# The first 480 words of a hand-written order, written anew, in an attention and gMLP kernel

## The chip, the core and the metric

The kernel runs on one core of a Trainium2 chip. The metric is the device time of one execution in microseconds (us). Six engines of the core work beside each other, each through its own list of instructions in order: TensorE (PE in the profile, its weight loads PEld), VectorE (DVE), ScalarE (ACT), GpSimd (POOL), SyncE (SP, which here only issues DMAs), and the DMA engines. They wait for each other by semaphores.

## What is computed

Attention over 8 batches of 12 heads, 448 positions and 64 dimensions, with q and k normalised by their root mean square, and behind it one gated block with a product over positions:

```
q_n, k_n = rmsnorm(q, g_q), rmsnorm(k, g_k)
attn = softmax(q_n @ k_n.T / 8);  x = attn @ v          # heads side by side: 8 x 448 x 768
h = relu(x @ w_in);  u, v = h[..., :512], h[..., 512:]
v_n = (v - mean(v)) / sqrt(var(v) + 1e-6)
out = (u * (w_spatial @ v_n + b_spatial)) @ w_out       # 8 x 448 x 768
```

Inputs and output are float32; the products are made in bf16 and summed in float32.

## The kernel before

A group G is four heads of one batch, so there are 24 groups, three to a batch. Nothing is scheduled by a program: `PLAN` is one string of 1632 words, and a loop at the end of the kernel function walks it and calls for each word the function `op_` of its first letter. A word reads name.arguments/slots/engine: `Q.1.1/2/g` squares k of group 1 (the last argument 0 is q, 1 is k) into buffer 2 on POOL (g; a is ACT, v DVE). Each engine runs its instructions in the order of the words that land on it, so the string decides what stands behind what.

The words that matter here, with the lines of the instructions:

- `l`, `L` (L306, L302): load a half of group 0's q or k, or q or k of another group, into one of nine buffers `raw`, issued by SP. `v`, `ws`, `wb`, `wo`, `wi` load v and the weights, issued by POOL. `g` loads a gain, issued by ACT.
- `q`, `Q` (L391 on DVE and POOL, L389 on ACT): squares. `r`, `R` (L409, L403, DVE only): row sums of the squares. `i`, `j` and `I`, `J` (L432, L435, L418, L425, ACT): the reciprocal root by a logarithm and an exponential. `n`, `N` (L450, L442): the normalised rows `nrm`. Small letters are the halves of group 0.
- `p`, `P` (L469, L461, PE): seven transposes by the identity into a PSUM bank. `k`, `K` (L372, L370 for q, L480, L478 for k with the gains): the copy out of it into `qT` or `kT`. From group 4 on `T` (L497), a DMA transpose, and `Z` take their place.
- `S.G.u` (L523, PE): two blocks of scores into two banks. With `f` it is four matmuls of 64 columns of weights, without it eight of 32. `E.G.u` (L532, ACT): the exponential of these two blocks into one of 21 buffers `et`; seven to a group.
- `s`, `a`, `b` (L558, PE): the sums of the exponentials and the two halves of their product with v. With a last argument 1 a word does two groups, eight matmuls. `D`, `d` (L577, L581, ACT) and `X` (L587, DVE) divide.
- `V`, `W`, `U` (L603, L637, L677, PE): products with w_in, and `c`, `u`, `B`, `H`, `G`, `O`, `o`, `t` the rest of the block.
- `Y`, `y` (L357 on PE, L372 on DVE or L370 on ACT): w_spatial transposed and copied. `gA` (L376, DVE), `gB` (L381, PE), `gC` (L384, DVE): the product of the two gains, turned into a column.
- `z.n.w` (L269, PE): n idle units, matmuls of the identity that nobody reads. Of them w times four make one wide matmul of 512 columns; the rest are narrow ones of 128 columns, or of 64 where the slot is `e`.

Operations of DVE and POOL that go through `port` (squares, norms, some copies) wait for the last such operation of the other engine that stands ahead of them in the plan. The order of the plan is kept on every engine, also where an operand comes late.

## Time and profile before

| | |
|---|---|
| runs | 265.84, 266.46, 266.88 us; median 266.46 |
| profiled execution | 268.54 us in all, span 266.7 us |
| mean granted TensorE clock | 0.985 |
| DMA | 51.08 MB, mean 192 GB/s |
| chain that ended last | PE 66%, DMA 11%, DVE 8%, ACT 7% |

The span goes from the first to the last instruction of the profiled execution. A busy PE says that some matmul was under way, not that it went at full speed. In the rows below, a time with a length is the start of a group of instructions and how long they took together, x the count, and in brackets the idle time of the engine ahead of them and what ended it. Where instructions of one engine overlap at their ends, the start of the next is the better measure of a length than the end.

### The profile page before, as it was taken

The page shows a single profiled execution, that of the slowest core. Times are in us where ns is not written, and L with a number is a line of the kernel's source. Part 1 is how long each engine was busy: PE and PEld are TensorE (multiplying, and loading weights), DVE is VectorE, ACT ScalarE, POOL GpSimd, SP SyncE. Part 2 cuts the span into 40 slices and gives each one's busy share as a digit, 9 for nine tenths or more (in the row PEclk, how much of TensorE's full clock was granted, in tenths as well). Part 3 has the DMA queues.
Part 4 walks back from the last instruction along what each step waited for, and adds up shares of the span by engine and source line. Part 5 has one row for each costly group of instructions (what it writes and reads, how often), then busy time and mean ns, then how long its engine had stood idle before and what let it go on. Part 6 is the DMA issues. An engine that isn't in the chain of part 4 may idle for free.

```text
span 266.7 us, 9428 instructions
## 1 busy us (share of the span) xinstructions
PE 254.9 (96%) x4025; PEld 129.4 (49%) x4041; DVE 213.3 (80%) x368; ACT 216.8 (81%) x357; POOL 127.5 (48%) x109
## 2 busy tenths in 40 slices
PE   7989999999999999999999999999999999999993
PEld 2454435434545456454455454454455555455561
DVE  4899799998698999979799988898983564476861
ACT  1788999999999999997899999997989983332522
POOL 3686246778874789267888577518210000000000
PEclk9995999999999999999999999999999999999999
DMA  6999997999999999999999999999952051031136
GB/s 194 328 306 312 225 258 98 161 232 222 147 233 288 226 240 187 329 204 186 238 240 223 211 248 182 180 196 264 228 115 118 2 209 32 2 124 57 29 158 227
DMA packets 62690, 51.08 MB, mean 192 GB/s; under 512 B 39160, under 2 KB 58808, under 8 KB 62648
## 3 DMA queue, kind: packets, MB, share of 16 engines
q1 hardware_dynamic: 54304, 42.02, 63.4%
q0 software_dynamic: 8192, 8.27, 20.2%
q8 instruction: 31, 0.51, 0.8%
q10 hardware_dynamic: 152, 0.20, 0.2%
q14 instruction: 11, 0.09, 0.1%
HBM read 38.55 MB, written 11.01 MB: 186 GB/s over the span
## 4 chain that ended last, share of the span: by engine, by line
PE 66%; DMA 11%; DVE 8%; ACT 7%; POOL 4%; issue 3%; SPq 0%; POOLq 0%; DVEq 0%
PE ps L558 13%; PE ps L677 11%; PE ps L523 10%; PE ps L713 10%; PE ps L603 9%; PE ps L691 7%; ACT et L532 5%; DMA raw<-in_q_dram 5%; PE ps L637 3%; DMA qT<-nrm 3%; DMA kr<-nrm 3%; POOL nrm L442 3%; DVE xt L587 1%; DVE ss L403 1%; POOL sqt L391 1%
## 5 line engine op out<-in xcount | busy, mean ns | idle before, releaser
L532 ACT ACTIVATE et<-ps 128x896 bf16<-128x896 f32 x168 | 145.3, 923 | 8.1 <-PE ps L523 7.3
L442 POOL TENSOR_TENSOR nrm<-raw,rs 128x896 bf16<-128x896 f32 x32 | 53.7, 1690 | 23.8 <-ACT rs L425 7.3
L391 POOL TENSOR_TENSOR sqt<-raw 128x896 f32<-128x896 f32 (+1 forms) x28 | 46.1, 1650 | 35.4 <-DVE sqt L391 20.1
L523 PE MATMUL ps<-qT,kT 64*32 64x448 bf16 (+1 forms) x1060 | 59.2, 361 | 2.7 <-DMA qT<-nrm 0.6
L403 DVE TENSOR_REDUCE ss<-sqt 128x14 f32<-128x896 f32 x46 | 49.0, 1077 | 1.2 <-POOL sqt L391 1.0
L558 PE MATMUL ps<-et,vt 64*32 64x448 bf16 x1344 | 44.8, 350 | 0.0
L677 PE MATMUL ps<-xt,w_in 128*128 128x448 bf16 x192 | 43.8, 353 | 0.1
L523 PEld LDWEIGHTS <-kT 64*32 64x32 bf16 (+1 forms) x1060 | 21.6, 94 | 33.6 <-issue 21.6
L713 PE MATMUL ps<-w_out,gt 128*128 128x384 bf16 (+1 forms) x196 | 37.5, 323 | 0.1
L603 PE MATMUL ps<-w_in,xt 128*128 128x512 bf16 x128 | 35.6, 380 | 1.0 <-issue 0.3
L587 DVE TENSOR_TENSOR xt<-ps,rc 128x448 bf16<-128x448 f32 x48 | 27.6, 615 | 7.8 <-PE ps L558 6.5
L370 ACT ACTIVATE os<-ps 128x384 f32<-128x384 f32 (+3 forms) x34 | 15.8, 477 | 16.1 <-PE ps L713 12.3
L558 PEld LDWEIGHTS <-vt 64*32 64x32 bf16 x1344 | 22.3, 92 | 12.0 <-issue 3.5
L691 PE MATMUL ps<-w_spT,vn 128*128 128x448 bf16 (+1 forms) x128 | 27.7, 353 | 0.1
L677 PEld LDWEIGHTS <-w_in 128*128 128x128 bf16 x192 | 17.5, 98 | 19.8 <-issue 5.3
L323 POOL DMA_DIRECT2D vt<-in_v_dram x36 | 24.0, 668 | 6.5 <-PE ps L523 6.5
L558 PE MATMUL ps<-et,ones 64*32 64x448 bf16 x672 | 25.9, 353 | 0.4 <-ACT et L532 0.4
L713 PEld LDWEIGHTS <-gt 128*128 128x128 bf16 x196 | 18.3, 98 | 16.0 <-issue 2.8
L372 DVE COPY os<-ps 128x384 f32<-128x384 f32 (+3 forms) x33 | 17.3, 535 | 10.7 <-PE ps L713 6.7
L696 DVE TENSOR_TENSOR gt<-ps,us 128x448 bf16<-128x448 f32 x32 | 19.5, 622 | 6.9 <-PE ps L691 6.1
L652 DVE BATCH_NORM_STATS2 s<-vs 128x6 f32<-128x512 bf16 (+1 forms) x32 | 21.8, 682 | 1.6 <-ACT vs L594 1.4
L603 PEld LDWEIGHTS <-xt 128*128 128x128 bf16 x144 | 12.7, 97 | 16.7 <-issue 5.4
(61 smaller groups left out, 255.8 us busy)
## 6 DMA issues: line engine op xcount, KB each, us to landing
raw<-in_k_dram SPq DMA_DIRECT2D x23, 448.0 KB, 6.1
raw<-in_q_dram SPq DMA_DIRECT2D x23, 448.0 KB, 5.7
out_dram<-os SPq DMA_DIRECT2D x23, 384.0 KB, 3.1
vt<-in_v_dram POOLq DMA_DIRECT2D x24, 112.0 KB, 5.8
vt<-in_v_dram POOLq DMA_DIRECT2D x12, 224.0 KB, 7.4
out_dram<-os SPq DMA_DIRECT2D x9, 192.0 KB, 4.3
w_in<-in_moe_w_in_dram POOLq DMA_DIRECT2D x1, 1536.0 KB, 14.1
w_out<-in_moe_w_out_dram POOLq DMA_DIRECT2D x4, 192.0 KB, 4.5
```

The source lines that it names most:

```text
L323: pool.dma_start(out=vts[b % 2][64 * halves[0]:64 * halves[0] + 64 * len(halves), g].rearrange("p r c d -> p r (c d)"), in_=src)
L391: port(eng, eng.tensor_tensor(out=t, in0=x, in1=x, op=ALU.mult))
L403: dve.tensor_reduce(out=sss[where["ssl", pair[G]]][:, G - pair[G], i].rearrange("p r c -> p (r c)"), in_=sqt[where.pop(("sq", G, i))].rear ...
L442: port(eng, eng.tensor_tensor(out=nrm[sl[0]].rearrange("p c r d -> p r c d"), in0=raw[where["raw", G, i]].rearrange("p r (c d) -> p r c d" ...
L523: pe.matmul(out=ps[at:at + w, sl[n], 0:S], lhsT=kT[64 * r:64 * r + 64, c, 64 * hh + x:64 * hh + x + w], rhs=qT[64 * r:64 * r + 64, :, 64 * ...
L532: act.activation(out=ets[sl[0]].rearrange("k n (p c) -> k n p c", c=C), in_=ps[:, a:a + 2, 0:S].rearrange("k n (c p) -> k n p c", p=T), fu ...
L558: pe.matmul(out=ps[32 * l:32 * l + 32, where[kind, G][0], 0:S], lhsT=w, rhs=et_of(G, r, c)[at:at + 64], start=(n == 1), stop=(n == C), til ...
L587: dve.tensor_tensor(out=xts[b % 2][:, 2 * g + half, :], in0=ps[:, where.pop(("ab"[half], G))[0], 0:S], in1=rcs[where["rc", G]], op=ALU.mult)
L603: pe.matmul(out=ps[:, bank, :], lhsT=xts[b % 2][:, j, 128 * m:128 * m + 128], rhs=w_in[:, j // 2, j % 2, DH:], start=(n == 1 and j == 2 * ...
L677: pe.matmul(out=ps[:, bank, 0:S], lhsT=w_in[:, j // 2, j % 2, 128 * f:128 * f + 128], rhs=xts[b % 2][:, j, :], start=(n == 1 and j == 2 * ...
L691: pe.matmul(out=ps[:, sl[0], 0:S], lhsT=vns[b % SLOTS["vn"]][rows, m, 128 * f:128 * f + 128], rhs=w_spT[rows, m, :], start=(m == 0), stop= ...
L713: pe.matmul(out=ps[:, sl[0], 0:n], lhsT=gts[b % 2][:, f, 128 * m:128 * m + 128], rhs=w_out[:, f, x:x + n], start=(f == 0), stop=(f == 3))
```

## The change

The first 480 or so words of `PLAN` are in another order; from word 486 on the names and engines are the same, with other buffer numbers. No function changes. The same operations are done, except for the idle units: `z.72.18`, twice `z.16.4`, `z.21.0`, `z.8.0` and `z.3.0` go, and `z.60.15`, `z.6.1`, `z.12.3`, `z.30.0`, `z.42.0` and `z.8.2` come, so 21 wide ones instead of 26, and 74 narrow ones instead of 32. 25 words change their engine or form, among them `n.1.0`, `n.1.1`, `n.0.1` (DVE to POOL), `k.1.1` (ACT to DVE), `k.1.0` (DVE to ACT), `k.0.0` (ACT to DVE), `Q.2.0` (POOL to ACT), `Q.1.0` (ACT to POOL), `Q.1.1` (POOL to ACT), `y.2` (DVE to ACT) and `N.1.0` (DVE to POOL). The start of the string:

```diff
-setup//v l.1.0/0 l.0.0/1 l.0.1 g.1//a g.0//a l.1.1 L.1.1/2 q.0.0/0/v r.0.0//v L.1.0/3 L.2.1/4 q.1.0/1/g r.1.0//v wb//g
-L.2.0/5 i.0//a j.0//a n.0.0//v z.72.18/0 p.0.0/0 q.1.1//a ws//g gA//v q.0.1//a k.0.0/0/a L.3.1/6 gB/7 n.1.0//v p.1.0/6
...
+setup//v l.1.0/0 l.0.0/1 l.1.1 g.0//a g.1//a l.0.1 L.1.1/2 q.0.0/0/v q.1.0/1/g r.0.0//v L.1.0/3 wb//g L.2.1/4 ws//g
+r.1.0//v q.1.1//a r.1.1//v i.0//a j.0//a n.0.0//v L.2.0/5 gA//v z.60.15/0 gB/0 L.5.0/6 q.0.1//a r.0.1//v gC//v L.3.1/7
...
```

What this does to ACT where the exponentials begin. Before, from the square of q of group 1 on (`et` with its number is an exponential, `kT0` the second half's copy of k, `ls` and `rs` the two small operations of group 1's norm):

```order
L389 ACTIVATE sqt1_74<-raw3_67 128x896
L532 ACTIVATE et0_90<-ps_63 128x896
L478 ACTIVATE kT0_86<-ps_63,g2_col_162 64x896
L532 ACTIVATE et1_91<-ps_63 128x896
L418 ACTIVATE ls0_116<-ss0_113,eps_157 128x28
L425 ACTIVATE rs0_119<-ls0_116 128x28
L532 ACTIVATE et2_92<-ps_63 128x896
```

Now, from the first half's copy of k on:

```order
L478 ACTIVATE kT0_86<-ps_63,g2_col_162 64x896
L389 ACTIVATE sqt0_73<-raw2_66 128x896
L532 ACTIVATE et0_90<-ps_63 128x896
L532 ACTIVATE et1_91<-ps_63 128x896
L532 ACTIVATE et2_92<-ps_63 128x896
L532 ACTIVATE et3_93<-ps_63 128x896
L418 ACTIVATE ls0_116<-ss0_113,eps_157 128x28
L425 ACTIVATE rs0_119<-ls0_116 128x28
L389 ACTIVATE sqt1_74<-raw5_69 128x896
L532 ACTIVATE et4_94<-ps_63 128x896
```

Four exponentials now stand in a row ahead of the norm of group 1, and the copy between the first two is gone.

DVE at the same place, before, from the copy of the gains on (`nrm01` and `nrm00` are the second halves' norms of group 0, `ss0` the row sums of group 1 and `ss1` those of group 2):

```order
L384 COPY g2_col_162<-ps_63 128x1
L480 TENSOR_SCALAR kT0_86<-ps_63,g2_col_162 64x896
L450 TENSOR_TENSOR nrm01_126<-raw0_64,rs0_124 128x448
L450 TENSOR_TENSOR nrm00_125<-raw1_65,rs0_124 128x448
L403 TENSOR_REDUCE ss0_113<-sqt2_75 128x14
L372 COPY qT0_80<-ps_63 64x896
L403 TENSOR_REDUCE ss0_113<-sqt1_74 128x14
L403 TENSOR_REDUCE ss1_114<-sqt0_73 128x14
```

Now:

```order
L384 COPY g2_col_162<-ps_63 128x1
L372 COPY qT0_80<-ps_63 64x896 x2
L480 TENSOR_SCALAR kT0_86<-ps_63,g2_col_162 64x896
L403 TENSOR_REDUCE ss0_113<-sqt0_73 128x14
L403 TENSOR_REDUCE ss0_113<-sqt1_74 128x14
L403 TENSOR_REDUCE ss1_114<-sqt2_75 128x14
```

Three copies out of PSUM now stand ahead of the first row sum of group 1, the norms have left the engine, and no row sum stands between the copies.

POOL, before, from its first load of v on:

```order
L323 DMA vt0_127<-in_v_dram 64x2x448
L391 TENSOR_TENSOR sqt2_75<-raw2_66 128x896
L343 DMA w_out_153<-in_moe_w_out_dram 128x768
L391 TENSOR_TENSOR sqt0_73<-raw4_68 128x896
L391 TENSOR_TENSOR sqt2_75<-raw5_69 128x896
```

Now:

```order
L323 DMA vt0_127<-in_v_dram 128x2x448
L450 TENSOR_TENSOR nrm01_126<-raw0_64,rs0_124 128x448 x2
L450 TENSOR_TENSOR nrm00_125<-raw1_65,rs0_124 128x448
L391 TENSOR_TENSOR sqt1_74<-raw3_67 128x896
L391 TENSOR_TENSOR sqt2_75<-raw4_68 128x896
L442 TENSOR_TENSOR nrm0_76<-raw3_67,rs0_119 128x2x7x64
```

Three half norms of group 0 have come to POOL, ahead of its squares, and one of its three squares has gone to ACT.

## The prediction

> **What bounds the kernel now.** I read the page's list of engines first, then the busy time by stage, then the engines in order of time up to 46 us, because the change touches nothing behind its 485th of 1632 plan words.

> ```profile
> PE 254.9 (96%) x4025; PEld 129.4 (49%) x4041; DVE 213.3 (80%) x368; ACT 216.8 (81%) x357; POOL 127.5 (48%) x109
> ```

> TensorE is the bound on average, but an average hides the stages. The next rows are the busy times by stage: for each stretch its length, then the busy time of PE, PEld, DVE, ACT and POOL, the granted clock, and the DMA's share and rate.

> ```profile
> 0.00:12.00 12.00, 9.70 (x50) 3.92 (x50) 7.00 (x20) 5.12 (x10) 5.90 (x12) 1.00 0.84 259
> 12.00:26.69 14.69, 13.42 (x193) 7.72 (x197) 13.58 (x19) 12.47 (x18) 10.89 (x9) 0.77 1.13 306
> 26.69:45.65 18.96, 17.43 (x465) 8.81 (x454) 17.52 (x22) 18.87 (x33) 7.39 (x7) 1.00 0.95 197
> 45.65:100.00 54.35, 54.06 (x892) 25.75 (x897) 49.21 (x88) 52.83 (x84) 42.11 (x34) 1.00 1.06 217
> ```

> From 45.65 to 100 us PE idles for 0.29 us, so whatever moves 45.65 moves the end by about as much. Ahead of it the bound is another: from 26.69 to 45.65 ACT idles for 0.09 us (18.96 less 18.87) and PE for 1.53. So I follow ACT's exponentials to 45.65, where the first matmul on w_in starts:

> ```profile
> 12.00 0.92 ACT L532 ACTIVATE et<-ps 128x896 bf16<-128x896 f32 x1 [0.30 <-PE ps L523]
> 12.94 1.00 ACT L478 ACTIVATE kT<-ps,g_col 64x896 bf16<-64x896 bf16 x1
> 15.30 0.32 ACT L418 ACTIVATE ls<-ss,eps 128x28 f32<-128x28 f32 x1 [0.41 <-DVE ss L403]
> 15.78 2.51 ACT L532 ACTIVATE et<-ps 128x896 bf16<-128x896 f32 x3
> 19.39 0.94 ACT L389 ACTIVATE sqt<-raw 128x896 f32<-128x896 f32 x1
> 20.23 3.55 ACT L532 ACTIVATE et<-ps 128x896 bf16<-128x896 f32 x4
> 23.93 0.92 ACT L532 ACTIVATE et<-ps 128x896 bf16<-128x896 f32 x1 [0.15 <-PE ps L523]
> 25.32 0.92 ACT L532 ACTIVATE et<-ps 128x896 bf16<-128x896 f32 x1 [0.47 <-PE ps L523]
> 26.57 2.73 ACT L532 ACTIVATE et<-ps 128x896 bf16<-128x896 f32 x3 [0.33 <-PE ps L523]
> 41.88 0.92 ACT L532 ACTIVATE et<-ps 128x896 bf16<-128x896 f32 x1
> ...
> 43.60 2.12 PE L558 MATMUL ps<-et,vt 64*32 64x448 bf16 x80
> 45.65 2.76 PE L603 MATMUL ps<-w_in,xt 128*128 128x512 bf16 x11
> ```

> Of the 28 exponentials of groups 0 to 3, nine are done at 23.78 (20.23 + 3.55), the last at 42.80, and 2.85 us later the w_in matmuls start. In a row each costs 0.80 ((2.51 - 0.92) / 2, three of them without the last one's length), and the two small operations of a norm cost 0.48 (15.30 to 15.78). I count 18.87 us from 23.93 to 42.80 for 19 exponentials and nine small operations, with 0.80 of waits for PE (0.47 + 0.33).

> Those waits have a cause. PE ran at half the clock from 19.86 to 26.69 us. I cut the time around it into pieces half as long as this stretch:

> ```profile
> 16.45:19.86 3.41, 2.33 (x53) 1.75 (x50) 3.11 (x5) 2.76 (x6) 3.39 (x5) 1.00 1.09 324
> 19.86:23.27 3.41, 3.33 (x40) 2.06 (x39) 2.86 (x5) 3.29 (x5) 2.19 (x2) 0.50 1.15 295
> 23.27:26.69 3.42, 3.42 (x40) 1.41 (x43) 3.42 (x7) 2.47 (x4) 2.20 (x2) 0.50 1.13 332
> ```

> And PE's groups (busy time and mean of one): of 16.45 to 19.86 the transposes of w_sp (L357) and all that are no transposes, of 19.86 to 23.27 the only one that is no transpose, and for comparison the idle units of 6.21 to 9.62, behind which the clock was kept:

> ```profile
> L357 PE MATMUL ps<-ident,w_sp 64*64 64x64 bf16 x28 | 0.7, 195 | 0.2 <-ACT et L532 0.2
> L269 PE MATMUL ps<-ident 128*128 128x64 bf16 x12 | 0.7, 194 | 0.0
> L523 PE MATMUL ps<-qT,kT 64*64 64x448 bf16 x4 | 0.6, 354 | 0.5 <-ACT et L532 0.5
> ...
> L523 PE MATMUL ps<-qT,kT 64*32 64x448 bf16 (+1 forms) x12 | 1.1, 559 | 0.1
> ...
> L269 PE MATMUL ps<-ident 128*128 128x512 bf16 x9 | 2.4, 396 | 0.0
> ```

> The clock was halved behind a piece with 1.3 us of matmuls that are no transposes (0.7 + 0.6) and was not given back behind one with 3.33 us of busy PE, of which only 1.1 were such matmuls. So I count matmuls without the transposes when I ask whether a stretch keeps the clock.

> **The change, step by step.** Engines run in order, so I walk the new order with these durations (PE's first, then DVE's, then POOL's):

> ```profile
> 1.69 6.27 PE L269 MATMUL ps<-ident 128*128 128x512 bf16 x18 [1.69 <-POOL ident masks.py:199]
> 9.46 1.04 PE L269 MATMUL ps<-ident 128*128 128x512 bf16 x4
> 10.89 1.06 PE L523 MATMUL ps<-qT,kT 64*32 64x448 bf16 x12 [0.40 <-DVE kT L480]
> 12.01 1.11 PE L469 MATMUL ps<-ident,nrm 128*64 128x128 bf16 x14
> 14.20 1.63 PE L523 MATMUL ps<-qT,kT 64*64 64x448 bf16 x28
> 15.76 0.79 PE L269 MATMUL ps<-ident 128*128 128x64 bf16 x21
> 21.41 1.09 PE L523 MATMUL ps<-qT,kT 64*64 64x448 bf16 x12
> 22.44 0.93 PE L461 MATMUL ps<-ident,nrm 128*128 128x128 bf16 x7
> ...
> 4.53 0.63 DVE L391 TENSOR_TENSOR sqt<-raw 128x448 f32<-128x448 f32 x1 [2.30 <-DMA raw<-in_q_dram]
> 7.45 0.62 DVE L450 TENSOR_TENSOR nrm<-raw,rs 128x448 bf16<-128x448 f32 x1 [0.62 <-ACT rs L435]
> 7.99 0.27 DVE L376 SCALAR_TENSOR_TENSOR g_row<-g_row 1x128 f32<-1x128 f32 x1
> 13.52 0.63 DVE L372 COPY qT<-ps 64x896 bf16<-64x896 bf16 x1
> 14.18 2.08 DVE L403 TENSOR_REDUCE ss<-sqt 128x14 f32<-128x896 f32 x2
> ...
> 9.62 1.68 POOL L391 TENSOR_TENSOR sqt<-raw 128x896 f32<-128x896 f32 x1 [1.45 <-DMA raw<-in_k_dram]
> 18.01 3.34 POOL L442 TENSOR_TENSOR nrm<-raw,rs 128x896 bf16<-128x896 f32 x2
> ```

> To 12.0 us nothing is won. n.0.0 still ends at 8.07; n.1.0 now runs on POOL behind it (half of 1.67, 0.85) to 9.0, the two transposes (0.55 each) end at 10.15, ACT copies k (1.00) to 10.7 and DVE copies q (0.63) to 10.8. The first scores start at 10.9 as before, so the first exponential starts at 12.0. The order of the first four loads changes, but before, POOL at 9.62 was the first engine behind n.0.0 to wait for a load, so the halves had landed by then. DVE does one half's row sum more ahead of n.0.0 than before (0.62, as the half's norm); if its load is there by 6.1, the sum fits ahead of 7.45. The price lies between nothing and 0.62, and I take nothing, since the second load was used at 4.53, 1.6 us ahead of it.

> From 12 to 16 us it loses. The two other transposes take 12.0 to 13.1. Their copies now stand both on DVE (0.63 each, to 14.4) and **ahead of the first row sum R.1.1**, which before ran meanwhile. DVE idles from 10.8 to 13.1, and the three sums (2.08 / 2 each) end at 17.4 where before the second and third ended at 16.26. PE does S.0.0 to 13.5, then 30 narrow idle units (0.79 / 21 each, 1.13 in all), then S.0.6, S.0.4 and S.0.5 from 14.65 to 15.9. ACT has done two exponentials at 13.75 and waits until 15.1: 1.35 us idle. The cover of that gap before was the copy k.1.1 on ACT, which the change takes away.

> From 16 to 24 us the loss stays. ACT: two exponentials to 16.85, the two small ones (0.48), the square Q.2.0 that was POOL's (0.84, 19.39 to 20.23) to 18.1, E.0.4 to 19.0, a wait for R.2.0 (DVE, 18.2 to 19.3), then y.2, which was DVE's (0.5 as an estimate, half of the 1.00 of a copy of twice the columns), two exponentials to 21.9, and Q.3.1 to 22.75. So seven exponentials are done at 22.75, where before nine were at 23.78: two behind, worth 1.6, and one microsecond ahead.

> PE: 42 narrow units (1.58) end at 17.5, the transposes of w_sp (0.7) at 18.2, then it waits for bank 0 (E.0.4) until 19.05. So in 16.45 to 19.86 its matmuls that are no transposes are 1.05 us of units and little of S.0.3, about as little as the 1.3 of before: I take the clock as halved again. Then two wide units (0.43 each at half clock as an estimate, between 0.35, the mean of the first 18, and twice the 0.26 of four at full clock) and P.1.1 (0.93 at half clock), behind N.1.1 on DVE (20.3), end at 22.1, its copy at 22.8, S.1.6 starts at 22.85 (before 21.41), S.1.4 follows, and E.1.4 starts at 23.95.

> From E.1.4 ACT has 21 exponentials instead of 19 and J.5.0 besides. So 23.95 + 18.87 + 1.60 + 0.16 (0.48 less 0.32, for J.5.0) = 44.6 with the same waits, 43.8 without. Behind the last exponential PE has to do 11 passes of eight matmuls (0.21 each by 2.12 / 10), 2.3 us, where before it was 2.85: 46.1 without the waits, 46.9 with them. By PE alone: the stretch from 21.41 to 45.65 was 24.24 us, less 1.53 idle, less 2.64 for half the clock to 26.69, leaves 20.07 of work; 22.85 + 20.07 + 1.92 + 1.53 = 46.37. The two ways agree between 46.1 and 46.9. I take 46.4, which is **0.75 us later** than 45.65.

> Behind 45.65 the edits cost nothing that I can see. POOL takes three squares (1.67 each) ahead of N.4.1, so the DMA transposes of group 4 are issued some 1.6 us later; cover is the six w_in passes (11 matmuls in 2.76) that now stand ahead of the first scores of group 4. If that cover is short, it costs up to 1.6; if PE's waits shrink by a third of the 1.53, 0.5 comes back.

> The sum stands against the profiled execution, 266.7 of span and 268.54 in all: 269.29. The runs shown have a median of 266.46, 2.08 lower, so 267.2.

> **The rivals.** (1) The clock holds. If the 42 units keep the clock up at 19.86, the wide units and P.1.1 take half: S.1.6 starts at 21.9, E.1.4 as soon as ACT is free, 22.75, and 22.75 + 18.07 + 1.76 + 2.3 = 44.9 (18.07 is 18.87 without the waits): 0.75 earlier than before, 265.7. For it speaks that narrow units are no transposes and fill a gap; against it that they end at 17.5, two thirds of a piece ahead of 19.86. [...]

> (2) Slower, by the front. Fifteen wide units end at 7.2 instead of 7.96 (three fewer, 0.26 each), and the product of the two gains, which now follows them, waits for gA on DVE (8.26). In 6.21 to 9.62 that leaves 1.0 us of units, some 0.3 of z.6.1 and a one-column product: about the 1.3 that lost the clock at 19.86, against 2.4 that kept it at 9.62. If it is lost, p.0.0 takes 0.4 longer (0.93 against 0.55), three wide units 0.5, the first scores between nothing (1.09 against 1.06) and 1.06, of which I take 0.5: 1.4, and every exponential from 12.0 on is late by it. 0.75 + 1.4 = 2.15, so 268.6; if the later 42 units, shifted into 16.45 to 19.86, then hold the clock there, 0.75 comes off: 267.9. [...]

> (3) The change doesn't do what it says. The order is said to fit the landings, but it moves loads too: L.3.0 now waits for a buffer of group 0. Before, these loads were issued well ahead and the exponentials of group 3 start behind 30 us, so I give it no price; then all stays at 266.5 if the lost exponentials are made up by the ACT work moved to DVE and POOL.

> **How the numbers follow.** Chances: forecast 0.5, clock holds 0.22, front 0.2, no effect 0.08. Half a per cent, 1.33 us (265.13 to 267.79), is about what a measurement of this kernel can tell from no change. The forecast's own bounds, 46.1 to 46.9, give 266.9 to 267.7, inside it; the clock's case, 265.7, passes 265.13 only if the later stage gives its 0.5 back and a little more; the front's case lies above. So 0.13 faster, 0.6 same, 0.27 slower, and a range of 265.5 to 268.6.

> **What would show it.** Right: ACT idle by over 1 us ahead of the third exponential near 15 us; R.1.1 behind two copies, near 14.3; seven exponentials done near 22.75; first w_in matmul near 46.4; clock 0.5 in two pieces. Wrong: w_in near 44.9, a clock that never drops behind 6 us (rival 1), or one that drops near 10 us (rival 2).

## The result: slower by 2.9%

The changed kernel takes 273.96 us (median of four runs, 273.0 to 276.01), the kernel before 266.57 on the same chip: a ratio of 1.029, 95% interval 1.023 to 1.036. The prediction was 267.2 with a range of 265.5 to 268.6.

The first rows of the profile after: the engines, then the four pieces of 3.4 us around the half clock (columns as before: length, PE, PEld, DVE, ACT, POOL, clock, DMA).

```profile
span 274.0 us, 9529 instructions
## 1 busy us (share of the span) xinstructions
PE 257.5 (94%) x4078; PEld 131.9 (48%) x4078; DVE 211.5 (77%) x363; ACT 217.7 (79%) x358; POOL 132.0 (48%) x113
```

```profile
12.84:16.26 3.42, 3.42 (x80) 2.26 (x79) 3.22 (x4) 2.42 (x4) 1.99 (x2) 1.00 1.16 283
16.26:19.67 3.41, 2.08 (x64) 1.76 (x63) 3.19 (x5) 2.97 (x7) 2.43 (x3) 1.00 1.06 350
19.67:23.08 3.41, 3.27 (x35) 1.79 (x31) 1.97 (x5) 2.80 (x5) 3.34 (x4) 0.50 0.99 254
23.08:26.50 3.42, 3.42 (x43) 1.94 (x36) 2.56 (x5) 2.65 (x4) 1.89 (x3) 0.50 1.12 322
```

PE has been busy for 2.6 us more in a span 7.3 longer, and the clock was halved for two pieces, as before. The walk through ACT in the new order:

```profile
12.10 1.73 ACT L532 ACTIVATE et<-ps 128x896 bf16<-128x896 f32 x2 [0.34 <-PE ps L523]
14.82 1.77 ACT L532 ACTIVATE et<-ps 128x896 bf16<-128x896 f32 x2 [1.00 <-PE ps L523]
...
19.92 1.72 ACT L532 ACTIVATE et<-ps 128x896 bf16<-128x896 f32 x2
21.52 0.96 ACT L389 ACTIVATE sqt<-raw 128x896 f32<-128x896 f32 x1
23.85 0.92 ACT L532 ACTIVATE et<-ps 128x896 bf16<-128x896 f32 x1 [1.37 <-PE ps L523]
...
42.97 0.95 ACT L532 ACTIVATE et<-ps 128x896 bf16<-128x896 f32 x1
```

So the exponentials go nearly as forecast: the third at 14.82 (15.1), seven done near 21.6, E.1.4 at 23.85 (23.95), the last of group 3 done at 43.92 (43.8 to 44.6). The loss is elsewhere. These are the first w_in matmul (L603) and all of PE's waits of over 0.25 us behind 42 us that name no engine and no DMA:

```profile
43.60 0.75 PE L558 MATMUL ps<-et,vt 64*32 64x448 bf16 x20 [0.68 <-issue]
47.88 0.37 PE L558 MATMUL ps<-et,vt 64*32 64x448 bf16 x5 [0.91 <-issue]
48.18 0.60 PE L603 MATMUL ps<-w_in,xt 128*128 128x512 bf16 x2
150.18 0.57 PE L523 MATMUL ps<-qT,kT 64*32 64x448 bf16 x15 [0.30 <-issue]
164.08 0.37 PE L558 MATMUL ps<-et,vt 64*32 64x448 bf16 x4 [0.54 <-issue]
180.91 0.38 PE L558 MATMUL ps<-et,vt 64*32 64x448 bf16 x7 [0.62 <-issue]
```

In the first profile of the kernel before no such wait stood there; the same group of the page has 0.0 us of idle time before the change and 2.7 after it:

```profile
L558 PE MATMUL ps<-et,vt 64*32 64x448 bf16 x1344 | 44.8, 350 | 0.0
```

```profile
L558 PE MATMUL ps<-et,vt 64*32 64x448 bf16 x1344 | 46.3, 350 | 2.7 <-issue 2.7
```

"Issue" is a wait for nothing that the profile shows. I numbered all of PE's rows in order of time from 0 (weight loads, matmuls, and the some 20 semaphore and drain rows among them): the waits end at rows 1217, 1473, 4801, 5313 and 5825, and each of these leaves 193 when divided by 256. The page has a DMA queue of the kind "instruction" with 31 packets before and 32 after, of 16 KB each:

```profile
q8 instruction: 31, 0.51, 0.8%
```

```profile
q8 instruction: 32, 0.52, 0.9%
```

PE reaches a row that leaves 193 as often as there are packets (31 times in e11, the second profile of before; 32 times after the change), so I read them as PE's own instructions arriving in pieces of 256 rows. The change adds 74 rows to PE's code (37 pairs of a weight load and a matmul, from the narrow idle units in front), so every later row stands 74 further on against these pieces. That is **theory P**: the position of the code costs the time. **Theory O**: the new order itself does, through the late exponentials and, near 76 us, through a transpose issued late behind N.8.0, which moved to DVE. **Theory C**: the half clock.

### The profile page after: what moved, and what is told of

It reads as the page before. It is cut to its first block, busy times and chain, and to the rows that moved or that the text cites. A ratio compares the mean times of both kernels' runs of the same rounds, so it can differ in the third digit from the quotient of the medians.

```text
span 274.0 us, 9529 instructions
## 1 busy us (share of the span) xinstructions
PE 257.5 (94%) x4078; PEld 131.9 (48%) x4078; DVE 211.5 (77%) x363; ACT 217.7 (79%) x358; POOL 132.0 (48%) x113
## 4 chain that ended last, share of the span: by engine, by line
PE 68%; DMA 12%; ACT 9%; DVE 5%; issue 3%; POOL 1%; SPq 0%; DVEq 0%; POOLq 0%; ACTq 0%
PE ps L558 15%; PE ps L677 12%; PE ps L523 11%; PE ps L603 9%; PE ps L713 9%; PE ps L691 8%; ACT et L532 6%; DMA qT<-nrm 3%; DMA kr<-nrm 3%; PE ps L637 2%; DMA raw<-in_q_dram 2%; DMA raw<-in_k_dram 2%; DMA out_dram<-os 2%; DVE ss L403 2%; POOL nrm L442 1%
## 5 line engine op out<-in xcount | busy, mean ns | idle before, releaser
L532 ACT ACTIVATE et<-ps 128x896 bf16<-128x896 f32 x168 | 145.4, 923 | 11.9 <-PE ps L523 11.2
L442 POOL TENSOR_TENSOR nrm<-raw,rs 128x896 bf16<-128x896 f32 x31 | 52.1, 1689 | 27.2 <-ACT rs L425 6.8
L391 POOL TENSOR_TENSOR sqt<-raw 128x896 f32<-128x896 f32 (+1 forms) x30 | 49.4, 1652 | 31.6 <-DVE sqt L391 12.8
L523 PE MATMUL ps<-qT,kT 64*32 64x448 bf16 (+1 forms) x1060 | 61.2, 361 | 3.1 <-ACT et L532 2.1
L403 DVE TENSOR_REDUCE ss<-sqt 128x14 f32<-128x896 f32 x46 | 49.0, 1077 | 2.8 <-ACT sqt L389 1.4
L558 PE MATMUL ps<-et,vt 64*32 64x448 bf16 x1344 | 46.3, 350 | 2.7 <-issue 2.7
L677 PE MATMUL ps<-xt,w_in 128*128 128x448 bf16 x192 | 43.8, 353 | 0.1
L523 PEld LDWEIGHTS <-kT 64*32 64x32 bf16 (+1 forms) x1060 | 22.2, 94 | 32.6 <-issue 23.8
L603 PE MATMUL ps<-w_in,xt 128*128 128x512 bf16 x144 | 37.6, 380 | 0.0
L558 PEld LDWEIGHTS <-vt 64*32 64x32 bf16 x1344 | 23.1, 92 | 16.0 <-issue 7.2
L370 ACT ACTIVATE os<-ps 128x384 f32<-128x384 f32 (+3 forms) x36 | 16.8, 478 | 17.5 <-PE ps L713 12.3
L691 PE MATMUL ps<-w_spT,vn 128*128 128x448 bf16 (+1 forms) x128 | 27.6, 353 | 0.0
L558 PE MATMUL ps<-et,ones 64*32 64x448 bf16 x672 | 26.0, 350 | 0.2 <-DVE us L596 0.2
L372 DVE COPY os<-ps 128x384 f32<-128x384 f32 (+3 forms) x31 | 16.3, 534 | 12.4 <-PE ps L713 6.6
L713 PEld LDWEIGHTS <-gt 128*128 128x128 bf16 x196 | 18.2, 98 | 15.8 <-issue 2.9
L603 PEld LDWEIGHTS <-xt 128*128 128x128 bf16 x144 | 12.7, 98 | 16.1 <-issue 4.7
```

The source lines that it names most:

```text
L391: port(eng, eng.tensor_tensor(out=t, in0=x, in1=x, op=ALU.mult))
L403: dve.tensor_reduce(out=sss[where["ssl", pair[G]]][:, G - pair[G], i].rearrange("p r c -> p (r c)"), in_=sqt[where.pop(("sq", G, i))].rear ...
L442: port(eng, eng.tensor_tensor(out=nrm[sl[0]].rearrange("p c r d -> p r c d"), in0=raw[where["raw", G, i]].rearrange("p r (c d) -> p r c d" ...
L523: pe.matmul(out=ps[at:at + w, sl[n], 0:S], lhsT=kT[64 * r:64 * r + 64, c, 64 * hh + x:64 * hh + x + w], rhs=qT[64 * r:64 * r + 64, :, 64 * ...
L532: act.activation(out=ets[sl[0]].rearrange("k n (p c) -> k n p c", c=C), in_=ps[:, a:a + 2, 0:S].rearrange("k n (c p) -> k n p c", p=T), fu ...
L558: pe.matmul(out=ps[32 * l:32 * l + 32, where[kind, G][0], 0:S], lhsT=w, rhs=et_of(G, r, c)[at:at + 64], start=(n == 1), stop=(n == C), til ...
```

## The experiments

Position 0 is that of the kernel before (4041 weight loads and as many matmuls, 8082 rows; 16 of the matmul records are missing from its first trace). The changed kernel, with 8156, is at +74.

**Undo the position in the changed kernel, make it in the kernel before.** Four edits:

```diff
e1, of after:   -z.42.0/e  +z.5.0/e                        (+74 -> 0)
e2, of before:  -z.72.18/0 +z.73.6/0                       (0 -> +74)
e3, of after:   -z.60.15/0 +z.61.3/0                       (+74 -> +148)
e4, of after:   -z.42.0/e  +z.36.0/e, +z.24.6/4 ahead of P.1.0 (+74)
```

> The changed kernel with 5 of the 42 narrow idle units behind Q.2.0 (37 pairs of a weight load and a matmul fewer), so that TensorE's later code stands again where the kernel before has it; before 266.6 us, after 274.0. Theory P (the 74 added rows shift TensorE's code against the pieces in which it is loaded, and TensorE stalls where a piece comes late): the stalls with no releaser at 42.9, 47.0, 149.9, 163.5 and 180.3 us go, the first w_in matmul comes near 46.5 instead of 48.2, and the time is 269.5 to 272. Theory O (the new order itself costs it, by ACT's late exponentials and by N.8.0 on DVE, behind which L.10.0 lands late): 273.5 to 274.5. If the missing units also cost the clock where it was kept, 1 us more by either.

> The kernel before with z.73.6 in place of z.72.18: 12 wide idle units become 49 narrow ones of about the same time, so TensorE has 74 rows more, as in the changed kernel, and nothing else moves. Theory P: stalls with no releaser appear at the same rows of TensorE's code as after the change (near 40 to 47, 147, 160 and 177 us) and the time is 268.5 to 270. Theory O: no such stalls, 266 to 267.3.

> The changed kernel with z.61.3 in place of z.60.15: again 37 pairs more in about the same time, so a third position of the code. Theory P: the five stalls of the changed kernel move or go, and the time differs from its 274.0 by over 1 us either way (271 to 273, or 275 and more where it hits more). Theory O: 273.5 to 274.5 with the stalls where they were in time or without any.

> The changed kernel with 6 wide idle units in TensorE's gap at 17.7 to 19.0 us (ahead of P.1.0) and 36 narrow ones instead of 42 ahead of it, so the code is as long as after the change. Theory C (the half clock at 19.7 to 26.5 costs 2 to 3 us of the lost time): the clock holds there, E.1.4 starts near 22.9 instead of 23.85, and the time is 271 to 272.5. Theories P and O: clock or not, the time stays within 0.7 us of 274.0, since ACT and the stalls behind set the end.

| | us (median) | against before, 95% | stalls at a row 193, profiled run |
|---|---|---|---|
| e1 | 270.65 | 1.011 (1.004 to 1.018) | none |
| e2 | 274.38 | 1.026 (1.018 to 1.033) | 1.20, 2.80, 0.48 |
| e3 | 269.16 | 1.009 (1.005 to 1.013) | 0.66, 2.16 |
| e4 | 273.47 | 1.020 (1.010 to 1.029) | 0.94, 0.63, 1.35, 0.34 |

e2 answers it. It is the kernel before with 12 wide idle units written as 49 narrow ones at 2 to 8 us, and it loses as much as the change does, and more than the 2 to 3.4 us that P expected. Its stalls, in the timeline of PE:

```profile
46.12 0.36 PE L558 MATMUL ps<-et,vt 64*32 64x448 bf16 x2 [1.20 <-issue]
...
163.72 0.37 PE L558 MATMUL ps<-et,vt 64*32 64x448 bf16 x4 [2.80 <-issue]
...
180.22 0.38 PE L558 MATMUL ps<-et,vt 64*32 64x448 bf16 x7 [0.48 <-issue]
```

They stand in the same matmuls as those of the changed kernel near 48, 164 and 181 us, and make up 4.48 of the 5.1 us by which its output units stand later than in the profile of before. That profile has the half clock, which e2 has not. Against e11, which kept the clock too, they stand 7.6 us later, of which 2.0 are there already when the last exponential of group 3, E.3.6, ends (42.00 against 40.02). In e1, at the old position, all five stalls are gone, as P said; its profiled run was the shortest of four, and the span is 267.0, against 266.7 for before with the same 6.8 us of half clock. e3 moved the later stalls away, but the third position gained 4.8 us where I had put 1 to 3; its profiled run was the longest of ten (272.18). e4 kept the clock (E.1.4 at 22.28) and kept the stalls; of its runs (270.88 to 277.44) the profiled one was the shortest. Theory C is not settled by it.

**How far the position may move, and from where it counts.**

```diff
e5, of after:   -z.42.0/e -z.30.0/e +z.29.0/e, +z.24.6/4 ahead of P.1.0 (0)
e6, of before:  -z.72.18/0 +z.72.14/0                      (+24)
e7, of before:  -z.72.18/0 +z.72.10/0                      (+48)
e8, of before:  +z.37.0/e ahead of S.13.1                  (0, then +74 from 124 us on)
```

> The changed kernel with TensorE's later code where the kernel before has it (74 rows fewer), and with six wide idle units (1.6 us) in the gap ahead of P.1.0 in place of the 42 narrow ones ahead of Y. Theory P (the position of TensorE's code is what the change lost by): no stall behind an instruction load, and the time is within 1 us of the kernel before, 265 to 267.5, if the clock holds at 19.7; 2 us more if it doesn't. Theory O (the new order itself loses over 1 us): 268 to 270.

> The kernel before with z.72.14 in place of z.72.18: 12 pairs (24 rows) more in front, in the same time. Theory P with a sharp edge (a load is asked for a fixed number of rows ahead, so a stall grows by some 0.027 us a row that its boundary stands earlier): 1 to 2 us slower than before, with one or two of the stalls of the 37-pair kernel at a third of their length. P with all or nothing: as before, or 7 us slower. Theory O: as before.

> The kernel before with z.72.10: 24 pairs (48 rows) more in front. P with a sharp edge: 3 to 5 us slower than before, between the kernels with 12 and with 37 pairs. Theory O: as before.

> The kernel before with 37 narrow idle units ahead of S.13.1, where TensorE waits 0.63 us for a transposed q at 125.2 us: 74 rows more, but only for the code behind that place. The units take 1.4 us, 0.8 more than the wait. Theory P: no stall at 45 us, but stalls near 161 and 180 us as in the kernel with 37 pairs in front (2.8 and 0.5), so 269 to 271. If what counts is the front (loads or order there), 267.3.

| | us (median) | against before, 95% | stalls at a row 193 |
|---|---|---|---|
| e5 | 270.72 | 1.009 (1.005 to 1.013) | 0.52, 1.82 |
| e6 | 271.85 | four runs from 267.17 to 272.81, no ratio | 1.53, 1.86, 0.42 |
| e7 | 272.12 | 1.013 (1.006 to 1.021) | 0.48, 1.81, 0.83 |
| e8 | 273.33 | 1.021 (1.014 to 1.028) | 0.58, 2.24, 1.31 |

e8 is the sharpest of them. Its front is that of before, the w_in matmuls start at 44.18, and the 37 units take 1.24 us where before PE waited 0.63. Then, 36 and 53 us further on, in work that the edit does not touch:

```profile
124.04 1.24 PE L269 MATMUL ps<-ident 128*128 128x64 bf16 x37 [0.47 <-ACT et L532]
...
161.21 0.37 PE L558 MATMUL ps<-et,vt 64*32 64x448 bf16 x4 [2.24 <-issue]
...
178.55 0.38 PE L558 MATMUL ps<-et,vt 64*32 64x448 bf16 x7 [1.31 <-issue]
```

In e8 the stalls of the later code came with the later code's position alone, behind the front of before; the time is above the 269 to 271 that P expected. e6 and e7 do not fit a sharp edge of 0.027 us a row (that figure was my estimate, and no run shows it): with 24 rows e6 has stalls of 1.53 and 1.86 us already (for the second the profile names DVE's `xt`, which ended 0.43 us ahead of PE), though the time of e7, 3.8 us above before, lies in the 3 to 5 expected. In e5 P expected no stall, and it has two. From the records of queue q8, and from PE's rows (us; the piece begins at the row 193 ahead):

```
kernel, row   piece begins  load starts  load ends   rows run out  goes on
after  1473        43.60       45.52       46.53        46.97       47.88
after  5313       160.14      161.20      163.25       163.53      164.08
after  5825       176.56      178.49      179.55       180.29      180.91
e8     5313       155.57      158.92      159.86       158.97      161.21
e8     5825       173.69      176.17      177.09       177.24      178.55
e11    5313       154.57      157.72      158.68       159.91      160.03
```

In these six rows a load starts 1.1 to 3.4 us after its predecessor's piece has begun, and PE goes on 2.3 to 2.9 us after the load's start. So a piece has to last some 4 to 6 us, as an estimate from these rows. With dense attention matmuls alone 256 rows last 3.4 us (3.37 and 3.39 in after, 3.40 in e8), and then PE ran dry in these rows; in e11, the kernel before, the same boundary falls where the piece ahead lasts 5.34 us, and PE waits 0.12.

A load that starts late is not the whole of it. In the table PE goes on 0.8 to 1.5 us after the load has ended, but in three stalls at row 1217, of e5, e6 and (below) e15, it does so only 2.8 to 3.2 us after it. In e5 the load ended at 42.25:

```profile
45.47 0.38 PE L558 MATMUL ps<-et,vt 64*32 64x448 bf16 x8 [1.82 <-issue]
```

POOL waits there too, 5.10 us without a releaser until 45.49. What held both is not shown.

**What is left of the order.** e1 and e5, at the old position, were still 1% slower than before. e9 holds the clock there by wide units; e10 moves it 24 rows further; the two kernels themselves were profiled again.

```diff
e9,  of after: -z.30.0/e +z.16.4/2, -z.42.0/e +z.25.0/e, +z.24.6/4 ahead of P.1.0 (0)
e10, of e9:    -z.25.0/e +z.13.0/e                                               (-24)
```

> The changed kernel with 74 rows fewer in another way: the 30 narrow idle units ahead of S.0.6 become 4 wide ones, of the 42 ahead of Y 25 stay, and 6 wide ones fill TensorE's gap ahead of P.1.0. The code behind stands where the kernel before has it, and the clock should hold from the front on. Theory P alone (the new order is neutral once the code's position and the clock are those of before): within 1 us of the kernel before. Theory O for the rest (the new order itself costs the 1% by which the two other kernels at this position are slower): 2.4 to 3.2 us slower than before.

> The same with 13 of the 42 narrow units: 24 rows fewer than the kernel before has. By the lengths of the pieces of 256 rows in the traces so far the positions 40 rows earlier to 0 are the best. P: as e9_phase_wide, within 0.7 us, and no stall of over 1 us at a piece's end. If the position of before is only lucky: 2 us or more slower than e9_phase_wide.

> The kernel before, unchanged, with a second profile. By P it has no stall of over 0.3 us at a row 193 of 256 in this profile either, whatever the clock did in the front; ratio 1.00.

> The changed kernel, unchanged, with a second profile. By P its stalls stand again at rows 1217, 1473, 4801, 5313 and 5825 or most of them, 2 to 5 us in all, though each one's length can differ, since the start of an instruction load varies by some microseconds; 273 to 275. If the delay of T.8.0 and L.10.0 at 70 to 80 us belongs to the order, it is there again (Q.10.0 1.7 us later against E.7.0 than before); if not, it is gone.

| | us (median) | against before, 95% | clock | stalls at a row 193 |
|---|---|---|---|---|
| e9 | 269.83 | 1.007 (1.002 to 1.012) | 0.996 | 0.74, 0.33 |
| e10 | 269.99 | 1.007 (1.002 to 1.011) | 1.000 | 0.23, 0.69, 0.19 |
| e11 (before) | 268.64 | 1.003 (0.999 to 1.007) | 1.000 | 0.43 |
| e12 (after) | 273.53 | 1.021 (1.013 to 1.029) | 0.997 | 0.32, 0.63, 1.42, 0.84 |

P had expected no stall of over 0.3 us in e11, which has one of 0.43. e9 stands 2.0 us above before, between what P (within 1) and O (2.4 to 3.2) expected. In e11 and e12 neither kernel lost the clock at 20 us, so the half clock belongs to the execution more than to the order. The two spans of the kernel before are 266.7 with it and 264.3 without, but that is not its price: ACT's square of k of group 3 (Q.3.1) starts at 19.39 in the first and at 17.75 in e11 (below), so 1.64 us were lost before the clock fell at 19.86. In the first, POOL's square of k of group 1 (Q.1.1) waited for its load until 9.62, and in e11 it started at 8.39. By 27.6 us, just behind the half clock, the distance is 2.82. So some 1.2 us, from this one pair, is what is left of theory C. The changed kernel stalls again at four of the five rows, and the late transpose near 76 us, which cost 1.5 us in the first profile of after, is gone: that part of theory O was one execution's. ACT around the start of the exponentials, before (e11), then after (e12):

```profile
11.47 0.92 ACT L532 ACTIVATE et<-ps 128x896 bf16<-128x896 f32 x1 [0.70 <-PE ps L523]
12.42 1.00 ACT L478 ACTIVATE kT<-ps,g_col 64x896 bf16<-64x896 bf16 x1
13.44 0.92 ACT L532 ACTIVATE et<-ps 128x896 bf16<-128x896 f32 x1
...
17.75 0.93 ACT L389 ACTIVATE sqt<-raw 128x896 f32<-128x896 f32 x1
...
20.61 4.23 ACT L532 ACTIVATE et<-ps 128x896 bf16<-128x896 f32 x5 [0.32 <-PE ps L523]
```

```profile
12.32 1.73 ACT L532 ACTIVATE et<-ps 128x896 bf16<-128x896 f32 x2 [0.34 <-PE ps L523]
15.04 1.77 ACT L532 ACTIVATE et<-ps 128x896 bf16<-128x896 f32 x2 [1.00 <-PE ps L523]
...
19.37 0.32 ACT L418 ACTIVATE ls<-ss,eps 128x28 f32<-128x28 f32 x1 [0.35 <-DVE ss L403]
```

From 11.5 us to the end of E.3.6 ACT idles for 0.46 us in e11 and 1.87 in e12, and E.3.6 ends at 40.02 and 42.22. The w_in matmuls follow:

```profile
43.63 2.76 PE L603 MATMUL ps<-w_in,xt 128*128 128x512 bf16 x12
```

```profile
45.85 2.76 PE L603 MATMUL ps<-w_in,xt 128*128 128x512 bf16 x12
```

These are 2.22 us, 0.52 of them stalls (0.95 less 0.43). So with the clock held the front of the new order costs 1.7 us in this pair. It is a pair that favours the old order: e11 is the shortest of its ten runs (266.11, median 268.64). In the profiles of the old order that kept the clock E.3.6 ends between 40.02 (e11) and 42.00 (e2, where Q.1.1 waited for its load until 9.66); in those of the new order with its own engines it ends between 41.48 (e10) and 43.30 (e3). The ranges overlap, so 1.7 is the value of one pair and not a price of the order. The two spans (264.3 and 270.3) differ by 6.0: 2.2 here, 0.4 given back by 150 us, 1.8 and 1.2 around rows 5313 and 5825, 0.1 behind, and 1.1 in the last copies, which wait for output DMAs. The last was there in all five profiles at 8156 rows (0.4 to 1.4 us: after, e2, e4, e8, e12) and in none of the others; each of the five has a 32nd instruction load that starts 7.8 to 8.8 us ahead of its end, but that this load is the cause was not shown.

**Which part of the front.** Two edits of e9 give ACT and DVE back their work; a third asks whether position 0 is one point.

```diff
e13, of e9:     -k.1.1//v +k.1.1//a
e14, of e13:    -Q.2.0/1/a, +Q.2.0/0/g ahead of N.1.0
e15, of before: -z.21.0/e +z.13.0/e, -z.8.0/e +z.4.0/e     (-24)
```

> The kernel e9_phase_wide (new order, TensorE's code where before has it, clock held) with the copy k.1.1 back on ACT. There the last exponential of group 3 ends 1.5 us later than in e11_before_again, with 1.88 us of ACT idle from 11.5 us on (0.46 there), 1.00 of it ahead of the third exponential. Theory A (the two copies on DVE ahead of R.1.1 cost it): the copy fills that gap, R.1.1 starts 0.6 earlier, and the last exponential of group 3 ends 0.3 to 0.6 us earlier than in e9. Theory B (the square Q.2.0 on ACT costs it): no earlier by over 0.2. By either the time stays within 0.8 us of e9_phase_wide, 0.3 to 0.9% slower than before.

> The same with the square Q.2.0 back on POOL too, in POOL's gap ahead of N.1.0 (2.5 us idle in e9_phase_wide). A and B together: ACT's idle time from 11.5 us to the last exponential of group 3 falls below 1.2 us, that exponential ends 1 to 1.5 us earlier than in e9, the first w_in matmul comes within 0.7 us of before, and the time is 0 to 0.5% above before. If the rest is not in the front (it is lost at the DMA transposes of 130 to 136 us), the w_in start comes earlier and the time does not follow.

> The kernel before with 12 narrow idle units fewer (z.13 and z.4 in place of z.21 and z.8), so TensorE's code stands 24 rows earlier, if the clock holds without them. P: as before within 0.4%, no stall of over 0.5 us at a row 193 behind 50 us. If any move of the code from the position of before costs: over 1 us slower.

| | us (median) | against before, 95% | E.3.6 ends | ACT idle to there | stalls at a row 193 |
|---|---|---|---|---|---|
| e9 | | | 41.49 | 1.64 | 0.74, 0.33 |
| e13 | 271.12 | 1.012 (1.003 to 1.021) | 42.34 | 1.39 | 0.40, 0.20 |
| e14 | 270.08 | 1.011 (1.002 to 1.019) | 42.05 | 1.93 | 1.48, 0.55 |
| e15 | 269.85 | 1.011 (1.007 to 1.015) | 41.14 | 1.59 | 1.16, 0.82 |

Neither theory A nor theory B of these expectations was borne out. With the copy back on ACT the gap shrinks from 1.00 to 0.50, but the copy takes 1.0 there, and E.3.6 ends 0.85 later; with the square off ACT too it is 0.56 later than in e9. So these profiles, one of each kernel, do not show the copy's move to DVE as a mistake by itself, and what in the front costs time stays open. e15 shows that position 0 is no broad plateau: 24 rows earlier the kernel before is 1.1% slower, with 1.98 us of stalls and, at 136 us, a wait of 1.50 for DVE's `us`, behind a transposed k that lands late. That wait is 0.59 in e11 and 0.98 to 1.27 in e1, e5, e9, e10, e13 and e14; what moves it I did not find. No kernel was faster than the one before.

e15 also gives a second position at which both orders were run. At -24 the new order is at 1.007 (e10) and the old one at 1.011 (e15); at +74 the new one is at 1.020 to 1.029 (the change, e4, e12) and the old one at 1.026 (e2). Only at position 0 does the new order stand behind, with 1.007 to 1.011 (e1, e5, e9) against 1.003 (e11), and the intervals of e9 and e11 overlap. So a cost of the order itself is not shown beyond that one position.

## Why the prediction was wrong

- *To 12.0 us nothing is won; then ACT idles 1.35; R.1.1 at 14.3.* Right: 12.10, 1.00, 14.35. P.1.0 waited until 18.99 as forecast (19.05), but for N.1.0 on POOL, not for a bank.
- *The clock is halved again, 19.86 to 26.69; S.1.6 at 22.85; E.1.4 at 23.95.* Right in that execution (19.67 to 26.50, 22.84, 23.85), but e12 kept it with the same order. I judged the clock of one execution as a property of the order.
- *The last exponential ends between 43.8 and 44.6, then 2.3 us of PE to the w_in matmuls.* The first part is right, 43.92. Then it took 4.26, since PE was behind by its two stalls (0.68 and 0.91): 48.18 instead of 46.4.
- *Behind 45.65 the edits cost nothing that I can see.* **This is the step that failed.** I looked for what the edits wait for and who waits for them, and not at the number of instructions. The 74 rows that the idle units add move all the code behind, and the position costs the kernel before 2.6% by itself (e2), 2.1% if moved only from 124 us on (e8, where 0.6 us is the units themselves). In e12 the four stalls cost 3.5 us with what hangs on them (0.5, 1.8 and 1.2) and, not shown to be their doing, the last copies 1.1. The squares on POOL, my one doubt there, stayed covered: PE had no wait near 49 us.
- *The sum against the profiled execution, less 2.08.* The term of the front rested on one execution, in which the front of before was itself late, by a load that landed later and by the half clock (ACT idle 2.60 from 11.5 us to the end of E.3.6, in e11 0.46), so the new order looked only 0.75 worse. Against e11 it is 1.7 worse, and the new order at position 0 is 0.7 to 1.2% slower than before. How much of this is the order stays open, as said above.
- The rivals: the clock did hold in e12, and the time was 272.4 instead of 265.7, for the same reason. The clock in the front was never lost, though in the first profile of after PE was busy for only 2.14 us of 6.02 to 9.43, with 1.25 us idle from 7.2 on. The 266.5 of rival 3 is out too, by the position of the code.

## What to carry to other kernels

Count the instructions that an edit adds or takes away on the busiest engine: here 74 rows moved everything behind against the pieces in which PE's instructions arrived and cost the kernel before 2.6% (e2), and a filler that nobody reads cost more than the gap it filled (e8: 1.24 us of units for a wait of 0.63 us, and 2.1% of the time). A wait without a releaser that returned at a fixed spacing of rows (here at rows that leave 193 by 256) was the sign, and an edit that changes only the count (a few narrow units for a wide one) was the test. Compare two orders at the same position, and take as a base an execution whose clock is that of most runs, and more than one: in the first profile of the kernel before Q.1.1 waited for its load until 9.62, and in e11 it started at 8.39.
